# A new order of steps for linear attention and an expert layer on one core, with the first products of zeros 63 x 64 instead of 8 x 504

## The chip, the cores and the metric

The kernel runs on one core of one Trainium2 chip. The metric is the time of one execution on the device in microseconds (us). Three runs of the kernel before gave 184.23, 184.34 and 184.44; the median is 184.34. The profile is of another execution, which took 184.03 us; its span, from the first to the last instruction of the program, is 182.3 us.

A core has five engines with a queue each: PE (matrix products; its weight loads are shown as PEld), DVE (vector), ACT (scalar functions), POOL (general purpose) and SP, which here only issues DMA transfers. An engine takes its instructions strictly in their order and stops at the first whose inputs are not there.

## The reference

Part one is a gated linear recurrence over 4 batches, 8 heads, 768 time steps and a head size of 48. A state S of 48 x 48 per head is kept:

```
state = alpha[t][:, None] * state + outer(k[t], v[t])
y[t]  = q[t] @ state
```

Part two takes all y as a matrix x of 3072 tokens x 384 and computes, with weights 384 x 2048 and 2048 x 384 and two scalars s and b,

```
h = x @ w_in;  r = max(h, 0);  g = s * r * r + b;  out = g @ w_out
```

Everything arrives and leaves as float32; the kernel multiplies in bfloat16. It computes r * r @ w_out, multiplies by s afterwards, and adds b times the column sums of w_out.

## The kernel before

**Tiles.** The 768 steps of a batch are cut into 6 chunks of 128, which makes 24 blocks n of 128 tokens. The first 8 blocks are handled in 4 pairs m (two chunks of one batch, names that end in 2); the inputs, logarithms and sums of decay of the others are also shared by two blocks. Part two works on 12 groups g of two blocks, and on 8 units u of 256 columns of the hidden layer (one `mm1` step is one unit for one group).

**An order written out by hand.** There are no loops over the work. The text `PROGRAM` lists small steps, and the last lines of the kernel function call them one after the other. Each step emits its instructions to the queue of its engine, so `PROGRAM` fixes the order on every queue, and also which engine does a step that several could do (the word DVE, ACT or POOL at its end) and which PSUM bank it uses. Waits between engines follow from the data. The steps that the text speaks of, with their line in the profile:

- `ld2.x.m` and `ld1.x.n` (L294, L283) load alpha (a), q, k or v; `ld_i.i` (L307) and `ld_o.i` (L320) load quarters of w_in and w_out, 768 KB each; all stand in SP's queue. `st` writes results.
- `ln2`, `cum2` and `blk2` (two and eight products on PE), `eb2`, `ei2`, `el2` (exponentials on ACT) make the running decay; `mul2.q.m.s` and `mul2.k.m.s` (L447) scale q and k with it; `vc2` (L335 or L333) converts v.
- `T2` (eight products, L459) (`T2.m.x.bank`, x = 0 for q and 1 for k) transposes q or k into a bank, and `Tc2` copies the bank into tile qkT. From block 8 on, `T1.n` (L616) does both by a transposing DMA transfer.
- `A2` (16 products, L496) multiplies k and q of a pair; `mk2` (L509, on DVE) masks the result into tile am. `KV2` (16 or 8 products, L481) makes the states; `t1` (DVE) and `sn` (mostly POOL) advance them. `y2` (L544 and L556, 76 or 88 products) makes y, and `ye` copies y into tile xd. `A1`, `KV1`, `Ayy` are the same for single blocks.
- `mm1.g.u.w` (6 products, L732) is x @ w_in for unit u of group g into bank h_ps of number w; `re` (L742 on ACT, L744 on DVE) is the relu, `sq` the square into tile gt. `mm2.n.jq` (4 products, L766) is a quarter of the second matrix for block n; `oe` (L775) scales and adds the bias on DVE.
- `cih.i.h` converts half a quarter of w_in to bfloat16 and `co.i` a quarter of w_out (L333, L335). `cp`, `ca`, `cf` (L359) add up the columns of w_out; `bsm` and `bmm` (L379) spread s, b and these sums over the partitions, `bc` makes the bias tile. `mm2.0` needs `co.0`, and `oe.0` needs `bc`.
- `F.n.w.to` (L824) issues n products of zeros, w columns wide, into a bank that nobody reads. They compute nothing.

Every product on PE is a weight load and a product. `c_...` steps set constants.

```
def F(n, w, to):
    for _ in range(n):
        nc.tensor.matmul(
            out=bank[to][:, 0:w], lhsT=zeros[:, 0:128], rhs=zeros[:, 0:w], start=True, stop=True
        )

ops = dict(locals())
for item in PROGRAM.split():
    name, *args = item.split(".")
    ops[name](*(int(x) if x.lstrip("-").isdigit() else x for x in args))
```

Of the kernel before, what the change touches and what calls it, by code (L numbers as in the profile page):

```python
# [59 lines left out]
re.2.7.1.1.DVE mm2.2.2 ld1.v.10 t1.7 A2.3.1.a mm2.2.3 ld1.q.8 mk2.3.1 mm1.2.2.0 ld1.q.9 oe.1 y2.3 blk2.4  # L60
ld1.v.8 ye.6.DVE ye.7.ACT mm2.3.0 re.2.2.0.0.ACT oe.2 cumA.4 ld2.a.5 sq.2.2.0.POOL mm2.3.1 st.0 ei1.9
ei1.8 mm1.3.5.1 mul1.k.9.DVE ld1.v.12 sq.2.7.1.ACT mul1.k.8.DVE mm1.3.7.0 el2.4 re.3.5.1.2.ACT ld1.q.13
sn.7.POOL mm2.3.2 eb1.8 re.3.7.0.0.ACT mul1.q.8.DVE mm1.3.4.1 ln2.6 sq.3.5.2.DVE T1.8 mm2.4.0
re.3.4.1.1.DVE vc1.8.POOL eb1.9 mm2.3.3 vc1.9.POOL st.1 mul1.q.9.DVE KV1.8 mm1.3.6.0 t1.8 T1.9 mm1.3.1.1
re.3.6.0.2.ACT sq.3.4.1.DVE sn.8.POOL KV1.9 ln2.5 mm2.4.1 oe.3 st.2 c_U sq.3.7.0.ACT t1.9 mm1.3.0.0
ld2.a.7 re.3.1.1.1.ACT sq.3.6.2.DVE blk2.5 mm2.5.0 ld1.q.12 sn.9.POOL ld1.q.14 cumA.5 sq.3.1.1.DVE A1.8
vc1.10.POOL eb1.10 mm1.3.3.1 mk1.8 ei1.10 mm2.5.1 ei1.11 re.3.0.0.0.ACT mul1.k.10.DVE mm2.5.2 eb1.11
mul1.q.10.DVE re.3.3.1.2.ACT mm2.5.3 sq.3.0.0.DVE T1.10 sq.3.3.2.ACT mul1.k.11.DVE mm1.3.2.0
mul1.q.11.DVE KV1.10 oe.5 mm2.4.2 re.3.2.0.1.ACT T1.11 t1.10 el2.5 mm2.4.3 ln2.7 sq.3.2.1.POOL A1.9 oe.4
ld1.k.13 mm2.7.0 sn.10.POOL mk1.9 st.4 mm2.6.0 ld1.k.12 mm2.7.1 st.3 Ayy.10 ld2.a.11 ld1.v.13 mm2.6.1  # L70
ye.8.DVE ye.9.ACT vc1.12.POOL mk1.10 mm2.7.2 ld2.a.8 mm1.4.1.1 blk2.6 mm1.4.2.0 re.4.1.1.0.ACT
sq.4.1.0.DVE cumA.6 ld1.v.11 re.4.2.0.2.ACT A1.11 mm1.4.4.1 ei1.12 sq.4.2.2.DVE eb1.12 mul1.k.12.DVE
mm2.7.3 el2.6 re.4.4.1.1.ACT mul1.q.12.DVE mm2.6.2 eb1.13 mk1.11 T1.12 mm1.4.3.0 sq.4.4.1.DVE mm1.4.0.1
re.4.3.0.0.ACT mul1.q.13.DVE ld1.q.15 mm2.6.3 vc1.13.POOL ld1.v.14 re.4.0.1.2.ACT sq.4.3.0.DVE mm1.4.6.0
ei1.13 sq.4.0.2.DVE oe.6 KV1.12 mm1.4.7.1 re.4.6.0.1.ACT mul1.k.13.DVE mm2.8.0 vc1.11.POOL t1.12 T1.13
mm1.4.5.0 sq.4.6.1.DVE oe.7 Ayy.12 re.4.5.0.0.ACT ld1.q.16 ld1.k.14 ld2.a.9 mm2.8.1 ye.10.DVE ye.11.ACT
st.5 re.4.7.1.2.ACT sq.4.5.0.DVE blk2.7 mm1.5.4.0 mk1.12 ld1.k.15 KV1.13 mm1.5.5.1 re.5.4.0.1.ACT
sq.4.7.2.DVE mm2.9.0 t1.13 re.5.5.1.0.ACT mm1.5.6.0 sq.5.4.1.DVE sn.13.POOL ld1.v.15 A1.13
re.5.6.0.2.ACT cumA.7 vc1.14.POOL mk1.13 mm1.5.3.1 ld1.v.16 eb1.14 ei1.14 mm1.5.1.0 re.5.3.1.1.ACT
sq.5.6.2.DVE mul1.q.14.DVE mm2.8.2 el2.7 re.5.1.0.2.ACT mul1.k.14.DVE mm2.8.3 eb1.15 sq.5.3.1.DVE T1.14  # L80
ei1.15 sq.5.1.2.DVE mm1.5.2.1 sq.5.5.0.DVE mm2.9.1 re.5.2.1.1.ACT st.6 mul1.k.15.DVE mm1.5.0.0 oe.8
mm2.9.2 re.5.0.0.2.ACT vc1.15.POOL st.8 mm1.5.7.1 st.7 sq.5.0.2.DVE sq.5.2.1.DVE KV1.14 ld1.q.17
mm2.10.0 re.5.7.1.0.ACT t1.14 ln2.8 mm2.10.1 mul1.q.15.DVE mm2.10.2 sq.5.7.0.DVE T1.15 sn.14.POOL Ayy.14
ld1.k.16 mm2.10.3 ye.13.ACT mk1.14 vc1.16.POOL ld1.k.17 ye.12.ACT ld1.q.22 mm2.9.3 ld1.v.22 oe.10
mm1.6.1.0 blk2.8 KV1.15 re.6.1.0.2.ACT mm1.6.4.1 sq.6.1.2.DVE mm1.6.3.0 t1.15 re.6.4.1.1.ACT A1.15 oe.9
sn.15.POOL cumA.8 ld2.a.10 mm1.6.0.1 eb1.16 ei1.16 mul1.q.16.DVE mm2.11.0 re.6.0.1.0.ACT mul1.k.16.DVE
mm2.11.1 eb1.17 sq.6.4.1.DVE T1.16 ei1.17 sq.6.0.0.DVE mm2.11.2 re.6.3.0.2.ACT mul1.k.17.DVE mm2.11.3
el2.8 mk1.15 st.9 mm1.6.2.1 ld1.k.18 ld1.v.17 oe.11 mm1.6.6.0 re.6.2.1.1.ACT KV1.16 mm2.13.0
sq.6.2.1.DVE re.6.6.0.0.ACT t1.16 mm1.6.5.1 mul1.q.17.DVE mm1.6.7.0 sq.6.3.2.DVE T1.17 sn.16.POOL Ayy.16
re.6.7.0.1.ACT ln2.9 ld1.q.18 mm2.12.0 ye.14.ACT ye.15.DVE ld1.q.19 re.6.5.1.2.ACT sq.6.7.1.DVE ld1.k.19  # L90
mm2.13.1 ln2.10 ld1.v.18 sq.6.5.2.DVE mm1.7.0.0 sq.6.6.0.DVE st.10 mk1.16 mm1.7.4.1 vc1.17.POOL
re.7.0.0.1.ACT mm2.13.2 re.7.4.1.2.ACT blk2.9 sq.7.4.2.DVE mm1.7.6.0 ld1.q.23 A1.17 re.7.6.0.0.ACT
cumA.9 mk1.17 mm2.12.1 ei1.19 ld1.v.19 eb1.19 mm1.7.1.1 el2.9 sq.7.0.1.DVE eb1.18 mm2.13.3 ei1.18
mul1.q.18.DVE re.7.1.1.2.ACT mm1.7.7.0 mul1.k.18.DVE sq.7.1.2.DVE T1.18 mm1.7.2.1 mul1.q.19.DVE
re.7.7.0.1.ACT mul1.k.19.DVE mm2.12.2 re.7.2.1.2.ACT sq.7.7.1.DVE mm1.7.3.0 ld1.q.20 ln2.11 oe.13
vc1.18.POOL ld1.k.20 mm2.12.3 sq.7.2.2.DVE re.7.3.0.1.ACT T1.19 mm2.15.0 oe.12 KV1.18 vc1.19.POOL
mm1.7.5.1 ld1.q.21 sq.7.3.1.DVE mm2.14.0 t1.18 st.13 re.7.5.1.2.ACT ld1.v.20 mm2.14.1 st.12 Ayy.18 st.11
ld1.k.21 mm2.15.1 ye.16.ACT ye.17.DVE sq.7.6.0.DVE KV1.19 mm1.8.5.0 sq.7.5.2.DVE mk1.18 mm1.8.6.1
re.8.5.0.1.ACT blk2.10 mm1.8.7.0 re.8.6.1.0.ACT t1.19 A1.19 sq.8.6.0.DVE re.8.7.0.2.ACT cumA.10
sq.8.5.1.DVE mm1.8.3.1 sn.19.POOL mk1.19 el2.10 ei1.20 eb1.20 mm2.14.2 re.8.3.1.0.ACT mul1.k.20.DVE  # L100
# [761 lines left out]
```

## Time and profile before

| | |
|---|---|
| median of three runs | 184.34 us |
| profiled execution, its span | 184.03 us, 182.3 us |
| PE busy, products | 171.9 us (94%), 2309 |
| DVE, ACT, POOL busy | 136.6, 103.8, 47.2 us |
| DMA | 34.96 MB, mean 192 GB/s |
| instruction queue q8 | 18 packets, 0.29 MB |
| granted PE clock | 1.00 throughout |
| fillers `F` | 21 products, 5.7 us busy |

A row of a group names line, engine, operation, the tile written and the tiles read. "Idle before" is the time in which the engine had nothing to do, with what ended it; "issue" there means that no event in the profile explains the wait. A window's row lists the busy time of each engine in a stretch of the span, and the share of the 16 DMA engines. The chain of work that ended last is followed back from the last instruction. Where a line has x16, 16 instructions are merged.

### The profile page before, as it was taken

The page shows a single profiled execution, that of the slowest core. Times are in us where ns is not written, and L with a number is a line of the kernel's source. Part 1 is how long each engine was busy: PE and PEld are TensorE (multiplying, and loading weights), DVE is VectorE, ACT ScalarE, POOL GpSimd, SP SyncE. Part 2 cuts the span into 40 slices and gives each one's busy share as a digit, 9 for nine tenths or more (in the row PEclk, how much of TensorE's full clock was granted, in tenths as well). Part 3 has the DMA queues.
Part 4 walks back from the last instruction along what each step waited for, and adds up shares of the span by engine and source line. Part 5 has one row for each costly group of instructions (what it writes and reads, how often), then busy time and mean ns, then how long its engine had stood idle before and what let it go on. Part 6 is the DMA issues. An engine that isn't in the chain of part 4 may idle for free.

```text
span 182.3 us, 5580 instructions
## 1 busy us (share of the span) xinstructions
PE 171.9 (94%) x2309; PEld 122.5 (67%) x2309; DVE 136.6 (75%) x257; ACT 103.8 (57%) x204; POOL 47.2 (26%) x79
## 2 busy tenths in 40 slices
...
GB/s 156 325 355 375 276 338 374 365 271 212 196 217 211 156 158 260 163 234 155 214 238 202 190 223 153 151 214 185 250 58 154 79 96 150 2 5 86 0 133 86
DMA packets 101357, 34.96 MB, mean 192 GB/s; under 512 B 94548, under 2 KB 99796, under 8 KB 101332
## 3 DMA queue, kind: packets, MB, share of 16 engines
...
q8 instruction: 18, 0.29, 0.6%
...
## 4 chain that ended last, share of the span: by engine, by line
PE 75%; DVE 10%; DMA 6%; SPq 3%; issue 3%; POOL 1%; ACT 1%; DVEq 0%; POOLq 0%
PE o_ps L766 31%; PE h_ps L732 28%; SPq L294 3%; DMA qkT<-qk 3%; PE a_ps L638 3%; DMA k_in<-in_k_dram 3%; DVE colsum L359 3%; DVE am L509 2%; PE py_ps L660 2%; PE ct_ps L660 2%; PE ct_ps L571 2%; PE py_ps L625 1%; POOL qk L447 1%; DVE t L701 1%; DVE r L744 1%
## 5 line engine op out<-in xcount | busy, mean ns | idle before, releaser
L732 PE MATMUL h_ps<-xd,w_in_bf 128*128 128x256 bf16 x576 | 74.2, 273 | 0.8 <-DVE r L744 0.6
L742 ACT ACTIVATE r<-h_ps 128x512 bf16<-128x512 f32 x87 | 51.8, 599 | 40.7 <-PE h_ps L732 36.8
L766 PE MATMUL o_ps<-w_out_bf,gt 128*128 128x384 bf16 x368 | 69.3, 326 | 0.1
L732 PEld LDWEIGHTS <-w_in_bf 128*128 128x128 bf16 x576 | 54.6, 98 | 13.7 <-issue 2.9
L766 PEld LDWEIGHTS <-gt 128*128 128x128 bf16 x368 | 34.3, 98 | 19.4 <-issue 0.9
L761 DVE TENSOR_TENSOR gt<-r 128x512 bf16<-128x512 bf16 x74 | 34.3, 484 | 13.4 <-ACT r L742 12.8
L711 POOL TENSOR_TENSOR s_st<-t,blast 128x384 bf16<-128x384 bf16 x15 | 14.6, 971 | 38.8 <-DVE t L701 35.8
L647 DVE TENSOR_TENSOR am<-a_ps,U 128x1024 bf16<-128x1024 f32 x16 | 19.5, 1219 | 3.8 <-PE a_ps L638 3.7
L335 POOL CAST vp<-v_in 128x384 bf16<-128x384 f32 x18 | 11.6, 646 | 33.4 <-DMA v_in<-in_v_dram 24.4
L775 DVE SCALAR_TENSOR_TENSOR o_sb<-o_ps,bs,bias_w 128x384 f32<-128x384 f32 x23 | 14.1, 613 | 3.8 <-PE o_ps L766 2.2
L759 ACT ACTIVATE gt<-r 128x512 bf16<-128x512 bf16 x18 | 11.1, 628 | 3.8 <-DVE r L744 3.7
L333 ACT ACTIVATE xd<-ct_ps 128x384 bf16<-128x384 f32 x6 | 2.9, 490 | 15.2 <-PE ct_ps L660 8.6
L394 ACT ACTIVATE la<-a_in 128x768 bf16<-128x768 f32 x12 | 10.1, 841 | 2.4 <-DMA a_in<-in_alpha_dram 2.4
L761 POOL TENSOR_TENSOR gt<-r 128x512 bf16<-128x512 bf16 x4 | 4.7, 1164 | 23.3 <-ACT r L742 12.3
L595 DVE TENSOR_TENSOR qk<-k_in,binv 128x384 bf16<-128x384 f32 x16 | 9.7, 612 | 1.2 <-ACT binv L585 1.1
L509 DVE TENSOR_TENSOR am<-a_ps,mask 128x1024 bf16<-128x1024 f32 x6 | 7.3, 1223 | 3.9 <-PE a_ps L496 3.7
L595 DVE TENSOR_TENSOR qk<-q_in,b_s 128x384 bf16<-128x384 f32 x16 | 9.7, 606 | 0.6 <-ACT b_s L581 0.4
L701 DVE TENSOR_TENSOR t<-py_ps,s_st 64x192 bf16<-64x192 f32 x26 | 9.2, 353 | 0.9 <-PE py_ps L625 0.5
L335 DVE CAST xd<-ct_ps 128x384 bf16<-128x384 f32 x6 | 3.3, 556 | 5.1 <-PE ct_ps L660 5.0
L447 DVE TENSOR_TENSOR qk<-q_in,b_s 128x384 bf16<-128x384 f32 x7 | 3.8, 556 | 4.3 <-ACT b_s L424 4.3
L824 PE MATMUL a_ps<-zeros 128*128 128x504 bf16 (+3 forms) x17 | 5.7, 478 | 1.3 <-DVE zeros L215 1.3
L333 ACT ACTIVATE xd<-py_ps 128x384 bf16<-128x384 f32 x8 | 3.9, 487 | 5.0 <-PE py_ps L660 3.6
...
## 6 DMA issues: line engine op xcount, KB each, us to landing
...
```

The costliest lines, as they stand in the source:

```text
L335: {"DVE": nc.vector, "POOL": nc.gpsimd}[eng].tensor_copy(out=out, in_=in_)
L509: nc.vector.tensor_tensor(out=o, in0=i, in1=mask2[s].rearrange("a t p -> a (t p)").unsqueeze(1).to_broadcast([128, n, 128]), op=ALU.mult,)
L595: on(eng).tensor_tensor(out=half_of(qk, n)[:, "qk".index(x), :, 0:D], in0=half_of(ins[x], n).rearrange("a (h d) -> a h d", d=D), in1=half_ ...
L647: nc.vector.tensor_tensor(out=half_of(am, n).rearrange("a e p t -> a (e p) t"), in0=a_ps.rearrange("a e (p t) -> a (e p) t", t=128), in1=U ...
L701: nc.vector.tensor_tensor(out=t1_sb[n % 2][r, :, w], in0=p_ps[r, :, w], in1=s_sb[(n - 1) % 4][r, :, w], op=ALU.add,)
L711: on(eng).tensor_tensor(out=s_sb[n % 4], in0=t1_sb[n % 2], in1=bl.unsqueeze(2).to_broadcast([128, NP, 96]), op=ALU.mult,)
L732: nc.tensor.matmul(out=h_ps[w][:, i * n : (i + 1) * n], lhsT=w_in_bf[:, kk, 128 * j : 128 * (j + 1)], rhs=xd_sb[g % 3][:, kk, 0:n], start= ...
L742: nc.scalar.activation(out=r_sb[i], in_=h_ps[w], func=AF.Relu)
L759: nc.scalar.activation(out=unit_out(g, u), in_=r, func=AF.Square)
L761: on(eng).tensor_tensor(out=unit_out(g, u), in0=r, in1=r, op=ALU.mult)
L766: nc.tensor.matmul(out=o_ps[n % 2][:, 0:d_model], lhsT=gt_of(n)[:, j, c0 : c0 + C], rhs=w_out_bf[:, j, :], start=(j == 0), stop=(j == NJ - 1),
L775: nc.vector.scalar_tensor_tensor(out=out_sb[n % 3], in0=o_ps[n % 2][:, 0:d_model], scalar=s_col, in1=bias_w, op0=ALU.mult, op1=ALU.add,)
```

## The change

Only `PROGRAM` changes; every function is the same. All 89 lines of it are written anew (90 after). The steps that compute are the same set, apart from engine, bank and buffer of some; the order moves within some microseconds everywhere. The fillers go from 8 x 504, 1 x 240, 3 x 480, 2 x 480, 2 x 296 and 5 x 456 to 63 x 64, 8 x 64, 4 x 384, 5 x 432, 6 x 480, 2 x 296 and 2 x 480 columns: 69 more products. In the head, one of q's multiplies moves from DVE to POOL, `vc2` steps move to ACT and POOL, half of a weight conversion moves from DVE to POOL, and k of pairs 1 and 3 is loaded earlier against v. Counted over the program, `re` goes from 87 on ACT and 9 on DVE to 89 and 7.

```
-c_U2 ln2.0 ld2.q.1 c_ident F.8.504.a0 cum2.0.0 c_vp.0 ld2.v.0 ln2.1 blk2.0 c_mask2 cum2.0.1 eb2.0.0
-cum2.1.1 ld2.k.1 mul2.q.0.0.DVE eb2.0.1 cum2.1.0 ei2.0.0 blk2.1 mul2.q.0.1.DVE el2.0 ei2.0.1
-mul2.k.0.0.DVE ld2.v.1 F.1.240.a0 T2.0.0.c eb2.1.1 mul2.k.0.1.DVE ei2.1.0 T2.0.1.y Tc2.0.0.c.ACT ld_i.1
-mul2.q.1.1.POOL el2.1 Tc2.0.1.y.DVE eb2.1.0 ld_i.0 vc2.0.0.POOL ei2.1.1 F.3.480.a0 A2.0.1.o vc2.0.1.ACT
-mul2.q.1.0.DVE A2.0.0.a c_s.0 mk2.0.1.0 ld_o.1 mul2.k.1.0.POOL mk2.0.1.1 F.2.480.c T2.1.0.o0 mk2.0.0
-KV2.0 mul2.k.1.1.POOL Tc2.1.0.o0.ACT ld2.a.2 t1.0 c_t1.1 vc2.1.1.ACT F.2.296.c T2.1.1.o1 vc2.1.0.ACT
-y2.0 Tc2.1.1.o1.DVE ld2.v.2 t1.1 A2.1.1.o ye.1.ACT A2.1.0.a ye.0.ACT sn.1.POOL mk2.1.0 cih.1.1.ACT KV2.1
-c_V2 cih.1.0.ACT mm1.0.3.0 t1.2 ld2.q.2 mm1.0.2.1 mk2.1.1.0 sn.2.POOL re.0.3.0.0.ACT mk2.1.1.1
-cih.0.0.ACT cih.0.1.POOL t1.3 sq.0.3.0.ACT ld2.k.2 c_ones sn.3.DVE re.0.2.1.1.ACT F.5.456.a0 y2.1
-cp.1.DVE ld_o.0 mm1.0.1.0 ye.2.ACT ye.3.DVE ln2.2 mm1.0.0.1 co.1.DVE ld_i.3 sq.0.2.1.ACT cum2.2.1
...
-T2.2.0.c Tc2.2.1.y.ACT mm1.1.1.1 co.0.POOL Tc2.2.0.c.DVE sq.1.3.2.ACT KV2.2 re.1.1.1.0.DVE A2.2.0.a
-re.1.0.0.1.ACT ld_o.2 cp.0.POOL mk2.2.0 mm2.0.0 sq.1.1.0.ACT cih.3.0.ACT mm2.0.1 t1.4 A2.2.1.a
-cih.3.1.ACT mm1.0.6.1 sq.1.0.1.DVE ld2.v.3 sn.4.POOL mk2.2.1 mm1.0.7.0 ld_bs re.0.6.1.2.ACT cih.2.1.DVE
-mm1.1.7.1 re.0.7.0.0.ACT cih.2.0.DVE sq.0.7.0.ACT mm1.1.6.0 ld2.k.3 ca.0.1.DVE re.1.7.1.1.ACT y2.2
...
-mul2.q.3.0.DVE el2.3 re.1.4.0.2.ACT KV2.3 ca.0.2.DVE T1.6 sq.1.4.2.ACT mm1.2.4.0 sq.2.6.1.ACT cf.DVE
-re.2.1.1.0.DVE bmm ld1.q.11 ld1.q.10 sq.2.1.0.POOL mm1.2.7.1 bc ld1.k.10 oe.0 mm2.1.0 ld1.k.11
...
+ln2.0 ld2.q.1 c_vp.1 c_t1.0 F.63.64.a0 cum2.0.0 c_vp.0 ld2.k.1 ln2.1 blk2.0 c_mask2 cum2.0.1 eb2.0.0
+cum2.1.0 ld2.v.0 mul2.q.0.0.DVE eb2.0.1 cum2.1.1 ei2.0.0 blk2.1 mul2.q.0.1.DVE el2.0 ei2.0.1 ld_i.1
+mul2.k.0.0.DVE F.8.64.a0 T2.0.0.c eb2.1.1 mul2.k.0.1.DVE eb2.1.0 ei2.1.0 T2.0.1.y ld2.v.1
+mul2.q.1.1.POOL el2.1 Tc2.0.0.c.ACT Tc2.0.1.y.DVE ld_i.0 mul2.k.1.0.POOL ei2.1.1 F.4.384.a0 A2.0.1.o
+A2.0.0.a mk2.0.1.1 mul2.k.1.1.POOL vc2.0.0.ACT ld2.a.2 mk2.0.1.0 vc2.0.1.ACT mul2.q.1.0.POOL mk2.0.0
+F.5.432.c KV2.0 T2.1.1.o1 c_t1.1 t1.0 c_s.2 T2.1.0.o0 ld_o.1 Tc2.1.1.o1.ACT c_V2 Tc2.1.0.o0.DVE y2.0
+cih.1.0.ACT t1.1 ld2.v.2 A2.1.0.a A2.1.1.o ye.1.DVE sn.1.POOL vc2.1.1.ACT mk2.1.1.0 ye.0.ACT c_ones
+mk2.1.1.1 vc2.1.0.ACT cih.1.1.ACT ld2.q.2 F.6.480.h0 KV2.1 mm1.0.2.1 t1.2 cih.0.0.ACT ld2.k.2 mk2.1.0
+sn.2.POOL re.0.2.1.0.ACT F.2.296.o1 mm1.0.0.0 ln2.2 cih.0.1.POOL mm1.0.3.1 t1.3 re.0.0.0.1.ACT
+sq.0.2.0.DVE y2.1 ld_o.0 re.0.3.1.2.ACT sn.3.DVE mm1.0.1.0 cp.1.DVE ye.2.ACT ld_i.3 ye.3.ACT cum2.2.1
...
+re.1.3.0.0.ACT mul2.k.2.1.DVE el2.2 sq.0.0.1.ACT mul2.q.2.0.DVE F.2.480.o1 T2.2.1.y ld2.a.3 sq.1.2.2.DVE
+T2.2.0.c Tc2.2.1.y.ACT mm1.1.1.0 co.0.POOL Tc2.2.0.c.DVE vc2.2.1.ACT re.1.1.0.1.DVE A2.2.0.a
+sq.1.3.0.ACT KV2.2 mk2.2.0 ld_o.2 cp.0.POOL re.1.0.1.2.ACT mm2.0.0 ld_bs cih.3.0.ACT mm2.0.1 t1.4
+A2.2.1.a cih.3.1.ACT sq.1.0.2.DVE mm1.0.6.0 ca.0.1.DVE ld2.k.3 sq.1.1.1.ACT mm1.0.7.1 re.0.6.0.0.ACT
+sn.4.POOL mk2.2.1 re.0.7.1.2.ACT mm1.1.7.0 cih.2.0.POOL sq.0.7.2.ACT mm1.1.6.1 ld2.q.3 re.1.7.0.1.ACT
+cih.2.1.DVE y2.2 re.1.6.1.2.ACT cp.3.DVE ld2.a.6 sq.1.7.1.ACT mm1.1.5.0 sq.1.6.2.POOL ye.4.DVE ye.5.ACT
...
+mm1.2.4.0 ca.0.2.DVE vc2.3.0.ACT re.1.4.1.1.ACT KV2.3 ld1.k.8 cf.DVE sq.2.5.0.ACT mm1.2.1.1 ld1.v.9 t1.6
+re.2.4.0.0.ACT ld1.v.13 bmm sq.1.4.1.ACT mm1.2.7.0 bc oe.0 mm2.1.0 re.2.7.0.1.ACT st.0 sq.2.4.0.ACT
...
```

More of the change, by code (lines that the diff above doesn't have):

```diff
@@ L60 @@
[L60 to L100, printed above, removed]
@@ new lines @@
+sq.0.2.0.DVE y2.1 ld_o.0 re.0.3.1.2.ACT sn.3.DVE mm1.0.1.0 cp.1.DVE ye.2.ACT ld_i.3 ye.3.ACT cum2.2.1
+co.1.DVE sq.0.3.2.ACT cum2.2.0 blk2.2 eb2.2.1 mm1.1.2.1 ld_i.2 re.0.1.0.0.DVE vc2.2.0.POOL ei2.2.0
+sq.0.1.0.DVE re.1.2.1.2.ACT mm1.1.3.0 mul2.q.2.1.DVE ld_o.3 ei2.2.1 mm1.1.0.1 eb2.2.0 mul2.k.2.0.DVE
+re.1.3.0.0.ACT mul2.k.2.1.DVE el2.2 sq.0.0.1.ACT mul2.q.2.0.DVE F.2.480.o1 T2.2.1.y ld2.a.3 sq.1.2.2.DVE
+T2.2.0.c Tc2.2.1.y.ACT mm1.1.1.0 co.0.POOL Tc2.2.0.c.DVE vc2.2.1.ACT re.1.1.0.1.DVE A2.2.0.a
@@ new lines @@
+sq.1.5.1.DVE re.0.4.0.0.ACT mm1.0.5.1 cp.2.DVE eb2.3.1 ld1.k.11 mm1.2.0.0 sq.0.4.0.ACT co.2.POOL
+re.0.5.1.1.DVE ei2.3.1 cum2.3.0 re.2.0.0.0.DVE bsm sq.0.5.1.ACT blk2.3 ld1.k.9 mm1.2.6.1 bsc eb2.3.0
+mul2.k.3.1.DVE mm1.2.5.0 ei2.3.0 mul2.q.3.1.DVE ld2.a.4 re.2.6.1.1.ACT mm2.0.2 sq.2.0.0.DVE T1.7 el2.3
+sq.2.6.1.ACT mul2.q.3.0.DVE mm2.0.3 mul2.k.3.0.DVE re.2.5.0.0.ACT mm1.1.4.1 ca.2.3.DVE T1.6 vc2.3.1.ACT
+mm1.2.4.0 ca.0.2.DVE vc2.3.0.ACT re.1.4.1.1.ACT KV2.3 ld1.k.8 cf.DVE sq.2.5.0.ACT mm1.2.1.1 ld1.v.9 t1.6
```

98 lines of the change are left out of this document (66 added, 32 removed).

## The prediction

> **What bounds the kernel now.** I read the windows view first, cut where the stages change, because the page's 94% for PE is an average. Columns: window, length, then busy time and count on PE, PEld, DVE, ACT, POOL, the granted clock, DMA share and rate.
>
> ```profile
> 0.00:12.00 12.00, 9.57 (x96) 4.78 (x98) 5.84 (x18) 7.50 (x15) 7.29 (x28) 1.00 0.95 261
> 12.00:18.16 6.16, 3.59 (x152) 2.68 (x151) 3.46 (x7) 4.18 (x7) 3.98 (x9) 1.00 1.05 384
> 18.16:22.80 4.64, 3.71 (x110) 2.60 (x106) 4.53 (x9) 2.38 (x5) 1.77 (x4) 1.00 1.02 277
> 22.80:30.07 7.27, 7.19 (x96) 5.50 (x89) 6.77 (x14) 7.22 (x15) 3.09 (x2) 1.00 1.05 353
> 30.07:34.80 4.73, 4.64 (x57) 3.20 (x50) 4.56 (x8) 4.12 (x8) 2.23 (x2) 1.00 1.07 366
> 34.80:46.92 12.12, 11.23 (x188) 8.68 (x187) 12.09 (x20) 11.11 (x23) 4.13 (x3) 1.00 0.97 253
> 46.92:179.25 132.33, 132.01 (x1638) 95.08 (x1638) 98.96 (x187) 67.28 (x134) 24.70 (x33) 1.00 0.74 155
> 179.25:182.30 3.05, 0.00 (x0) 0.00 (x0) 0.41 (x1) 0.00 (x0) 0.00 (x0) 1.00 0.32 110
> ```
>
> From 46.92 us on PE has no hole: whatever brings it there earlier with the same work done is kept to the end. Before that four things take turns. DMA is full (share about 1) from the first transfers to 47 us; DVE is full from 18 to 47 us; PE does little until 22.8 us. Then the chain of work that ended last, between 14 and 48 us (start, length, what):
>
> ```profile
> 15.39 2.09 issue
> 17.48 0.31 PE a_ps L496 x5
> ...
> 46.30 0.57 DVE colsum L359
> 46.92 0.93 PE o_ps L379 x2
> 47.87 0.63 DVE bias_w L384
> ```
>
> PE stops for 2.09 us inside `A2.1.0.a`, after 11 of its 16 products, waiting for nothing that a semaphore would show; and DVE's sum of the weight columns (`cf`) releases `bmm` at 46.92. The DMA view of 15.2 to 15.4 us names the first:
>
> ```profile
> q8 instruction: 1, 0.02, 29.9%
> ```
>
> The queue of instructions moves one packet there, its first; the page has 18 with 0.29 MB, 16 KB each. Over PE's 4618 loads and products that is 63 bytes each, so a packet holds some 256 of them, 128 load-product pairs. Before the stall stand 223 pairs, so a block begins at pair 224; its packet ran from 15.28 to 16.23 and PE went on at 17.48. The next block begins with pair 352, the third product of `mm1.0.1.0`, whose packet ran at 20.8: there too PE slipped 0.1 us. Read as "a block is asked for when the one before it is entered", pair 96 (`KV2.0`, 11.97) asks and 17.48 receives: 5.5 us; next 17.48 to 23.13: 5.65 us.
>
> The DMA floor of this stage shows on POOL, and PE follows it at `mm2.0.0`:
>
> ```profile
> 26.98 2.58 POOL L335 CAST w_out_bf<-gt 128x1536 bf16<-128x1536 f32 x1 [5.39 <-DMA gt<-in_moe_w_out_dram]
> 29.52 1.81 POOL L359 TENSOR_TENSOR colsum<-gt 128x768 f32<-128x768 f32 x1
> ```
>
> **The change, part by part.** The 2288 products that compute something (2309 less 21 fillers) are the same; the rest is order, engines and fillers.
>
> *Fillers.* 8 of 504 and 63 of 64 are both 4032 columns. The old ones start 0.42 us apart (0.83 ns a column), so 64 columns are 53 ns, and 63 end near 4.8 us as now; `cum2.0.0` waits for `ln2.0` until 5.07. That needs a weight load to pass in less than 53 ns. Nearest row: `blk2.0`, 8 pairs from 5.64 to 5.84, 25 ns a pair. Bounds 0 (as there) and +3.4 us (63 loads in series at the 114 ns mean of their rows, 7.2 us); I take 0. `F.8.64` (8 x 25 to 53 ns, 0.2 to 0.4 us) begins at 7.11 like `F.1.240`, and nothing needs PE until 7.55: 0. `F.4.384` (0.64) replaces `F.3.480` (0.6), covered by the wait for qkT until 10.16. `F.5.432` (0.9) waits out `v`. `F.6.480.h0` (6 x 0.2 = 1.2) and the two later ones are costed below.
>
> *Blocks of instructions.* 55 more pairs at the start put the boundary at pair 224 into `y2.0` (40th product, near 14.1 us) and its request at `T2.0.0.c` (7.55). 7.55 + 5.5 = 13.0: the stall goes. The next boundary falls on the 18th product of `y2.1`: 14.1 + 5.65 = 19.7; the third on `mm1.1.1.0`: 20.3 + 6.0 (23.13 asked, packet at 26.95 + 0.9, 1.3 to use) = 26.3. Both are just in time by the sums below. The Trainium skill ("Runtime: NRT & Kernel Launch", Instruction fetch mechanics) says that blocks of 256 are fetched while the one before runs and that crossing is mostly hidden. By that rule moving boundaries would be worth 0; the trace agrees on the blocks and shows 2.09 us at the first crossing.
>
> *SP.* k.1 passes v.0, and the first w_in slice passes v.1. By landing times (q.1 9.0, next 10.2, 11.4) k.1 lands at 10.2 instead of 11.4, v.0 at 11.4; w_in slice 1 at 13.5 instead of 14.6, v.1 14.6 instead of 12.6. Everything to `ld_o.0` is the same set, so the POOL row above stays at 26.98. Later k.3, q.3 pass v.3 (about 1.1 us each); v.3 is needed last.
>
> *POOL, ACT and DVE, 9 to 20 us.* POOL takes q.1.0 from DVE: four multiplies of 0.99 from 9.18 end at 13.15. `T2.1.0.o0` ends at 13.75, `y2.0` 14.8 (now 14.8), `A2.1` both halves 15.45 (now 17.8). ACT then has Tc2 1.0, cih.1.0 0.8, vc 0.5, ye 0.5, vc 0.5 in a row from 13.35: 16.5. `F.6.480` covers that and ends at 16.7, so it costs 0.2. `KV2.1` ends 17.15 (now 18.1), `mm1.0.2` 17.85; the next waits for w_in slice 0 (landing 18.04, cast 0.8): 18.85 to 20.15 for two; `F.2.296` is hidden there. DVE's t1.3 ends near 19.8, so `y2.1` runs 20.15 to 21.3, now 22.80, and three `mm1` are done instead of two: 1.5 + 0.65 = 2.15 us ahead.
>
> *20 to 30 us.* `T2.2` waits for k.2 (lands about 24.9) and four DVE multiplies, so `F.2.480` is free; `KV2.2` and `A2.2.0` end near 28.4, now 30.07. Then `mm2.0.0` needs POOL's cast: 26.98 + 2.58 = 29.56. The lead is 0.5 us, and 1.2 us of the gain turn into a wait for that cast.
>
> *30 to 47 us.* DVE loses work: cih.2.0 to POOL (0.6), vc2.2 and vc2.3 elsewhere, `ye` and `sq` about even. In before DVE runs from 30.18 to 46.87 without a hole. In the new order `ca.0.1` follows POOL's sum (31.33), then `mk2.2.1` ends at 33.45, and what follows to `cf` adds up, in start-to-start times, to 11.8 (casts 2.7, column sums 4.0, three relus 1.9, four multiplies 1.9, the rest 1.3), with a 0.2 wait for `y2.2`: 45.5 against 46.87. On PE, `y2.2` ends at 35.15; ten `mm1` 6.55, two `mm2` 1.3, the rest 1.9 and a 0.7 wait for a relu on DVE give 45.6. So `bmm` starts 1.3 us earlier, if every estimate holds; I take 1.0, between this and the 0.5 at 30 us.
>
> *From 47 us.* Same PE work (132.0 us), relus 2 more on ACT. Counted in PE work, the nearest `mm2` behind its last `mm1` moves from 1.5 to 2.1 us, the shortest lead of a transpose over its reader from 4.4 to 4.7. I take 0. The end is the same 3.05.
>
> Sum: 184.03 (profiled; span 182.3) - 1.0 = 183.03. The median shown, 184.34, is 0.31 above that execution: **183.3 us**.
>
> **The rivals.** *More is kept:* the wider distances also remove holes after 47 us. PE's steps there run 0.65 per six or four products; at that pace the work is some 129.7, so 2.6 us are slack; half of it gives 182.0.
>
> *Nothing is left:* DMA pins `cf` through `ld_o.2` (landing 36.8) and k.3, q.3, and DVE, still full, stays where it was. For it: DMA share 0.97 to 47 us. Against: none of its four sums starts on a landing in before. 184.2.
>
> *The small products are paced by their loads (slower):* then the first stage ends 3.4 us later; `mm2.0.0`, 1.2 us early for its cast, would be 1.7 late against now, and DVE's saving returns 0.3: 185.7. It decides from about 90 ns a pair. Against it: 25 ns a pair at 5.64. The Trainium skill ("TensorE: Matmul & The Clock Gate", LDWEIGHTS) has a load take columns / 1.2 ns, 107 ns here. By that rule alone 63 of them would last 6.7 us, and the sum would be near this rival's; the 25 ns row speaks against it.
>
> *Late transposes (slower):* the chain holds one qkT transfer of 5.27 us at 80.7, which cost PE 0.38 at 85. The leads of T1.14 and T1.20 shrink from 5.4 to 4.7 us of PE work; five such transfers would each cost 0.5: 2.5 - 1.0 = +1.5, 185.8. It decides when transfers take over 4.9 us.
>
> **How the numbers follow.** Forecast 0.44 (its own range 182.8 to 184.0), more kept 0.20, nothing left 0.13, paced by loads 0.08, late transposes 0.15. A change under 0.2% (0.37 us) can't be told from none here. Faster: 0.44 less 0.02 near the edge, plus 0.20 and a little of "nothing left": 0.65. Within: 0.11. Slower: 0.24. The range leaves out the far half of both slower cases: 181.9 to 185.3.
>
> **What would show it.** No 2 us issue hole near 15 us in PE's timeline, `A2.1` done by 15.6; the first instruction packet at 8 to 12 us; `mm2.0.0` at about 29.6 behind POOL's cast; `bmm` at 45.6 to 46.4; PE busy throughout behind it. Wrong if `cum2.0.0` starts after 5.5, a new issue hole over 0.5 us stands in `y2.1` or `mm1.1.1`, or holes after 47 us add up to over 1.3 us.

## The result, and the profile after

The changed kernel takes 186.94 us (median of 20 runs, 185.22 to 189.84), the kernel before beside it 184.74 us: a ratio of 1.0108, with a 95% interval of 1.0082 to 1.0133. It was forecast 1.0 us faster and is about 2 us slower. The profiled execution took 187.66 us, its span is 185.9 us. Every line number is one higher than before, since `PROGRAM` has one line more. In all tables below a median takes in every execution, while the ratio compares only those in the record's fast state, so that a median can stand higher than its ratio says (g1, where two of twelve are left, and i2, where five are).

The windows of the changed kernel, with the columns of the prediction's first fence:

```profile
12.00:17.11 5.11, 4.62 (x148) 3.22 (x148) 4.87 (x10) 3.67 (x8) 4.39 (x12) 1.00 1.07 355
...
20.00:29.24 9.24, 8.18 (x173) 6.36 (x173) 8.28 (x15) 8.58 (x18) 2.76 (x4) 1.00 1.00 311
...
33.96:46.05 12.09, 11.14 (x187) 8.60 (x187) 11.91 (x20) 10.79 (x23) 3.02 (x2) 1.00 1.06 275
46.05:103.15 57.10, 53.05 (x650) 36.11 (x651) 39.48 (x75) 29.55 (x61) 13.22 (x19) 1.00 1.04 192
103.15:182.85 79.70, 79.65 (x988) 58.86 (x988) 55.49 (x110) 39.22 (x77) 9.98 (x14) 1.00 0.54 121
```

The head came out as worked out in this execution: PE is busy 4.62 of 5.11 us where the stall of 2.09 us was. `bmm`, the end of the head, starts at 46.05 (before: 46.92). The loss stands in the row from 46.05: PE is idle for 4.05 of 57.1 us between `bmm` and `Ayy.14`; before, it was idle for 0.32 us from `bmm` to the end of its work (the prediction's row of 46.92 to 179.25), 0.22 of them in front of `Ayy.12`. Behind 103 us it is full again. The chain of work that ended last names the holes (start, length, what):

```profile
81.76 5.34 DMA qkT<-qk
87.15 0.40 PE a_ps L639 x8
87.55 0.51 PE py_ps L661 x28
88.18 4.29 DMA qkT<-qk
92.51 0.40 PE a_ps L639 x8
...
97.23 5.88 DMA qkT<-qk
103.15 0.40 PE a_ps L639 x8
```

These are the transposing transfers T1.12, T1.13 and T1.14; each time PE goes on 0.05 us behind the landing. Another hole waits for T1.6, whose reader `A2.3.0.a` (L497) starts at 50.23 after 0.45 us of idle time. The view of waits (engine, line, what it waited for: us in total, times, longest) adds up those of the single blocks, first of the kernel before, then of the changed one:

```profile
PE a_ps L638 <- DMA qkT<-qk: 0.2, 1, 0.2
```

```profile
PE a_ps L639 <- DMA qkT<-qk: 3.5, 3, 1.8
```

Why they are late shows in SP's queue, first of the kernel before, then of the changed one (start, length of the issue; L616 and L617 are `T1`, L283 and L284 `ld1`, L294 and L295 `ld2`, L815 and L816 `st`):

```profile
80.69 3.34 SPq L616 DMA_TRANSPOSE qkT<-qk  x1
84.08 0.58 SPq L283 DMA_DIRECT2D q_in<-in_q_dram  x1
84.75 0.53 SPq L283 DMA_DIRECT2D v_in<-in_v_dram  x1
85.39 1.64 SPq L616 DMA_TRANSPOSE qkT<-qk  x1
...
94.02 1.39 SPq L616 DMA_TRANSPOSE qkT<-qk  x1
```

```profile
81.76 2.98 SPq L617 DMA_TRANSPOSE qkT<-qk  x1
84.79 1.22 SPq L816 DMA_DIRECT2D out_dram<-o_sb  x2
86.06 0.59 SPq L284 DMA_DIRECT2D q_in<-in_q_dram  x1
86.69 1.38 SPq L816 DMA_DIRECT2D out_dram<-o_sb  x2
88.18 1.30 SPq L617 DMA_TRANSPOSE qkT<-qk  x1
89.52 2.67 SPq L284 DMA_DIRECT2D k_in<-in_k_dram  x3
92.23 0.97 SPq L284 DMA_DIRECT2D v_in<-in_v_dram  x1
93.24 1.82 SPq L284 DMA_DIRECT2D q_in<-in_q_dram  x2
95.11 0.70 SPq L284 DMA_DIRECT2D v_in<-in_v_dram  x1
95.86 1.26 SPq L284 DMA_DIRECT2D k_in<-in_k_dram  x1
97.23 1.92 SPq L617 DMA_TRANSPOSE qkT<-qk  x1
```

The multiplies that T1.13 reads end at 83.37, a microsecond earlier than before (84.42). But SP stands behind T1.12, st.4, q.15 and st.5 and issues it at 88.18. T1.14 is ready at 95.78, issued at 97.23 behind eight loads, and lands at 103.11. Four of these loads (k.16, k.17, q.16, q.17) are read 10 us later or more; before, only q.16 of them stood in front.

### The profile page after: what moved, and what is told of

The parts are those of the page before. It is cut to its first block, busy times and chain, and to the rows that moved or that the text cites. A ratio compares the mean times of both kernels' runs of the same rounds, so it can differ in the third digit from the quotient of the medians.

```text
span 185.9 us, 5717 instructions
## 1 busy us (share of the span) xinstructions
PE 174.2 (94%) x2378; PEld 125.9 (68%) x2378; DVE 132.8 (71%) x252; ACT 105.8 (57%) x208; POOL 45.8 (25%) x80
## 4 chain that ended last, share of the span: by engine, by line
PE 61%; DMA 15%; SPq 11%; DVE 7%; ACT 2%; issue 2%; DVEq 0%; ACTq 0%
PE o_ps L767 25%; PE h_ps L733 24%; DMA qkT<-qk 11%; SPq L295 8%; DMA wst<-in_moe_w_in_dram 4%; PE a_ps L639 3%; SPq L321 2%; PE py_ps L661 2%; DVE colsum L360 2%; PE ct_ps L572 2%; PE ct_ps L661 2%; SPq L308 1%; DVE qk L448 1%; PE py_ps L626 1%; PE ct_ps L416 1%
## 5 line engine op out<-in xcount | busy, mean ns | idle before, releaser
L743 ACT ACTIVATE r<-h_ps 128x512 bf16<-128x512 f32 x89 | 52.4, 597 | 40.7 <-PE h_ps L733 32.3
L762 DVE TENSOR_TENSOR gt<-r 128x512 bf16<-128x512 bf16 x74 | 32.3, 452 | 9.6 <-ACT r L743 9.1
L712 POOL TENSOR_TENSOR s_st<-t,blast 128x384 bf16<-128x384 bf16 x15 | 14.0, 934 | 62.0 <-DVE t L702 39.5
L336 POOL CAST vp<-v_in 128x384 bf16<-128x384 f32 x17 | 9.8, 585 | 25.2 <-DMA v_in<-in_v_dram 11.4
L596 DVE TENSOR_TENSOR qk<-q_in,b_s 128x384 bf16<-128x384 f32 x16 | 8.8, 553 | 2.9 <-ACT b_s L582 2.8
L639 PE MATMUL a_ps<-qkT 64*128 64x128 bf16 x128 | 6.3, 218 | 3.5 <-DMA qkT<-qk 3.5
L639 PEld LDWEIGHTS <-qkT 64*128 64x128 bf16 x128 | 4.0, 94 | 7.6 <-DMA qkT<-qk 4.9
L336 DVE CAST xd<-py_ps 128x384 bf16<-128x384 f32 x5 | 2.8, 556 | 5.8 <-PE py_ps L661 5.2
L825 PEld LDWEIGHTS <-zeros 128*128 128x128 bf16 x90 | 5.3, 121 | 2.3 <-DVE zeros L216 1.3
```

Of the source, the lines that this page charges most:

```text
L336: {"DVE": nc.vector, "POOL": nc.gpsimd}[eng].tensor_copy(out=out, in_=in_)
L596: on(eng).tensor_tensor(out=half_of(qk, n)[:, "qk".index(x), :, 0:D], in0=half_of(ins[x], n).rearrange("a (h d) -> a h d", d=D), in1=half_ ...
L639: nc.tensor.matmul(out=a_ps[:, e, 128 * p : 128 * p + 128], lhsT=T[r, 1, p, :], rhs=T[r, 0, p, :], start=True, stop=True,)
L712: on(eng).tensor_tensor(out=s_sb[n % 4], in0=t1_sb[n % 2], in1=bl.unsqueeze(2).to_broadcast([128, NP, 96]), op=ALU.mult,)
L743: nc.scalar.activation(out=r_sb[i], in_=h_ps[w], func=AF.Relu)
L762: on(eng).tensor_tensor(out=unit_out(g, u), in0=r, in1=r, op=ALU.mult)
```

## The experiments

Theory S: the transposes are late because loads that are not urgent stand in front of them in SP's queue. Theory D: DMA is full up to 110 us, so a PE that comes early waits there in any order, and a reorder only moves the hole. All kernels compute the same; "SP" in a diff means the order in SP's queue.

### Fillers and SP's order exchanged whole

```diff
 e1: the changed kernel; SP from T1.6 to T1.17 in the order of before
 e2: the kernel before; SP from T1.6 to T1.17 in the changed order
 e3: the changed kernel
-F.63.64.a0 ... F.8.64.a0
+F.8.504.a0 ... F.1.240.a0
 e4: the kernel before
-F.8.504.a0 ... F.1.240.a0
+F.63.64.a0 ... F.8.64.a0
```

> The changed kernel, with SP's queue between T1.6 and T1.17 in the order of the kernel before; every other queue as changed. Theory A (the new SP order issues loads ahead of the transposing transfers while DMA is full, so T1.12 to T1.14 land late): the 3.5 us of PE waiting for qkT shrink to under 1 us, Ayy.14 starts near 99 instead of 103, and the time falls from 186.9 to 183.5 - 185. Rival B (the new order on DVE, ACT and PE makes the operands of the transposes late, whatever SP does) and rival C (the 69 additional products of zeros): 186.5 - 187.5, holes as they are.

> The kernel before, with SP's queue between T1.6 and T1.17 in the new order; every other queue as before. Theory A: 186.5 - 188, with waits for qkT of 2 - 4 us at A1.12 to A1.14. Rivals B and C: 184.7 within 0.4.

> The changed kernel, with its first two fillers as before (8 x 504 and 1 x 240 columns in place of 63 x 64 and 8 x 64). Theory A: 186.9 within 0.7, the wait for qkT stays; the stall for the first block of instructions comes back (some 2 us near A2.1 or KV2.1), of which at most 0.5 reaches bmm, because POOL's cast pins mm2.0.0 near 29.5. Rival C: 184.7.

> The kernel before, with its first two fillers as changed (63 x 64 and 8 x 64 columns). Theory: the 2.09 us hole in A2.1.0.a goes, y2.1 starts 1 - 2 us earlier, bmm 0 - 0.9 us earlier, and the time is 0 - 0.9 us less: 183.8 - 184.7. Rival C: over 186.

| kernel | us (median, range) | ratio to before, 95% |
|---|---|---|
| e1 | 189.01 (188.38 to 190.45) | 1.0191 (1.0145 to 1.0237) |
| e2 | 191.34 (188.93 to 191.91) | 1.0270 (1.0207 to 1.0334) |
| e3 | 185.43 (184.77 to 187.37) | 1.0002 (0.9968 to 1.0035) |
| e4 | 184.43 (183.61 to 186.17) | 0.9960 (0.9923 to 0.9996) |

e1 missed its expectation, and e2 is far worse than the changed kernel. A whole queue order under another order of the multiplies makes other loads late: in e1 v.11 is issued at 83.66 instead of 69.68, in e2 v.16 at 103.02 instead of 92.69. SP's order is matched to the order of its readers, so these two say nothing on single transposes. e4 shows the fillers alone: the stall in `A2.1` is gone, `bmm` starts at 46.63, and the kernel is 0.4% faster by its ratio (on this group's ratios see below). e3 spoke against theory S, since it has the transposes and loads of the changed kernel and was not slower; it is taken up again below.

### Head and rest exchanged; transposes moved ahead

```diff
 f0: the changed kernel itself
 f1: the changed order up to re.2.5 (43 us), all that is left as in before
 f2: before up to re.2.5, all that is left as in the changed order
 f3: the changed kernel, SP:
-st.2 T1.9 ... ld2.a.9 ld2.a.8 T1.12 st.4 ld1.q.15 st.5 T1.13
+T1.9 st.2 ... T1.12 st.4 T1.13 ld2.a.9 ld2.a.8 ld1.q.15 st.5
-ld1.k.14 ld1.k.16 ld1.k.15 ld1.v.14 ld1.q.17 ld1.q.16 ld1.v.15 ld1.k.17 T1.14 st.6 T1.15
+ld1.k.14 ld1.k.15 ld1.v.14 ld1.v.15 ld1.q.16 T1.14 st.6 T1.15 ld1.k.16 ld1.q.17 ld1.k.17
```

> The changed kernel itself, so that the runs of this group and the one with the old fillers stand beside it on one chip. Theory S (transposes stand too far back in SP's queue of the changed order, whatever the head does): 186.9 us, ratio 1.008 to 1.013, holes in front of Ayy.12, A1.13 and Ayy.14 that add up to 2.5 to 4 us. Theory D (the DMA rings are full until 110 us, so a PE that comes early only waits there, in any order): the same 186.9, but the hole's place differs from execution to execution. Theory T (it is the phase: the order is sound and only one unlucky overlap of loads and transposes made it slow on that chip): 184.5 to 185.7.

> The changed order up to the 43rd microsecond (the relu of unit 5 of group 2), and behind it all that is left in the order, on the engines and in SP's order of the kernel before. Theory S: the head's 0.9 us are kept and the holes go: 183.3 to 184.1 against 184.7 for before, ratio 0.991 to 0.997; no hole over 0.7 us behind 47 us. Theory D: the lead is waited away at the transposes: ratio 0.998 to 1.003. Theory T: 0.99 to 1.01, no prediction.

> The other half: the kernel before up to the same step, and behind it the changed order with its engines and SP's order. Theory S: the holes stay and the head's 0.9 us are missing: 187 to 188.5, ratio 1.013 to 1.020. Theory D: a head that is 0.9 us late eats only slack, 186.5 to 187.2, ratio 1.009 to 1.013. Theory T (as with the old fillers, which also gave a late head): 185 to 185.8, ratio 0.998 to 1.004.

> The changed kernel with one thing different: in SP's queue T1.9 stands ahead of st.2, T1.12 and T1.13 ahead of the loads of alpha 9 and 8, of q.15 and of st.5, and T1.14 ahead of the loads of k.16, q.17 and k.17, whose readers come 10 us later; all other queues are as they were. Theory S: T1.12 is issued at 80.5 instead of 81.8, T1.13 at 83.5 instead of 88.2, T1.14 near 95.8 with fewer loads in front; the holes of 1.5, 0.5 and 2.0 us shrink to under 0.8 us together: 183.5 to 185.0, ratio 0.994 to 1.002. Theory D: loads that are pushed back make other readers late: 186 to 188, ratio 1.006 to 1.017, with holes at v, k or alpha in place of those at the transposes.

| kernel | us | ratio |
|---|---|---|
| f0 | 186.80 (184.92 to 187.92) | 1.0072 (1.0033 to 1.0112) |
| f1 | 184.74 (183.61 to 188.10) | 0.9973 (0.9937 to 1.0008) |
| f2 | 187.02 (185.49 to 193.09) | 1.0080 (1.0051 to 1.0109) |
| f3 | 186.14 (184.98 to 188.31) | 1.0062 (1.0028 to 1.0096) |

The whole loss is in the order behind 43 us: with the old order there (f1) it is gone, and with the old head and the new rest (f2) it is all there. With or without the new head, the new rest costs the same, so nothing of the head's microsecond shows in the end. Against the expectations, f1 stands between the two theories, f2 below both theories, and f3 in the interval of theory D.

f3's profile shows both theories at work. The transposes came out as meant; here is its SP queue:

```profile
81.02 1.29 SPq L617 DMA_TRANSPOSE qkT<-qk  x1
...
83.91 1.24 SPq L617 DMA_TRANSPOSE qkT<-qk  x1
...
94.64 1.57 SPq L617 DMA_TRANSPOSE qkT<-qk  x1
```

From `bmm` to `Ayy.14` it takes 52.62 us, against 57.10 in the changed kernel and 55.49 in f0. But then v.16, pushed behind three loads, is late, and PE waits for its conversion on POOL (timeline of f3):

```profile
108.69 0.77 POOL L336 CAST vp<-v_in 128x384 bf16<-128x384 f32 x1 [3.05 <-DMA v_in<-in_v_dram]
...
109.52 0.33 PE L626 MATMUL py_ps<-vp,qk 128*128 128x96 bf16 x4 [0.66 <-POOL vp L336]
```

`Ayy.14` to `A1.17` takes 19.83 us instead of 18.05, so that 1.8 of the 2.9 us won against f0 are given back.

### The give-back mended, the dose given to before

```diff
 g2: f3, SP:
-T1.15 ld1.k.16 ld1.q.17 ld1.k.17 ld1.k.18 ld1.v.22 ld1.v.16
+T1.15 ld1.v.16 ld1.k.16
 (T1.16 ahead of a.10 and k.18; T1.17 ahead of q.19; T1.18, T1.19 ahead of q.22, v.21;
  v.22, k.23 behind T1.19)
 g3: the kernel before, SP:
-T1.14 st.6 st.8 st.7 ld1.q.17 T1.15 ld1.k.16 ld1.k.17
+ld1.q.17 ld1.k.16 ld1.k.17 T1.14 st.6 st.8 st.7 T1.15
 g4: e4, SP:
-ld1.q.14 T1.10 ... ld2.a.11 ld1.v.13 ld2.a.8 ld1.v.11 T1.12
+T1.10 ... ld1.v.11 T1.12 ld1.v.13 ld2.a.8
 (T1.14 ahead of v.16; T1.16 and T1.17 ahead of k.18; a.11 behind T1.13)
 g1: f1, SP:
-ld2.k.1 ld2.v.0
+ld2.v.0 ld2.k.1
```

> As f3 (transposes ahead in SP's queue of the changed kernel), but the stretch from 98 to 125 us is mended too: v.16 directly behind T1.15, T1.16 ahead of the loads of alpha 10 and k.18, T1.17 ahead of q.19, and the loads of v.22 and k.23, whose readers come 40 us later, behind T1.19. f3 had cured Ayy.12 and Ayy.14 and then lost 1.8 us between A1.15 and A1.17 (14.7 us against 12.9). Theory S (a transpose is late because loads that are not urgent stand in front of it, and their order can be mended): Ayy.14 at most at 100.3, A1.15 to A1.17 12.9 to 13.3 us, 184.2 to 185.3, ratio 0.994 to 1.001. Theory D (the rings are full, and every reorder only moves the hole): 185.7 to 187, ratio 1.003 to 1.010, with holes of over 0.7 us at another reader.

> The kernel before with one thing different: in SP's queue T1.14 stands behind the loads of q.17, k.16 and k.17, as in the changed order, instead of ahead of them. Theory S: T1.14 is issued near 96.2 instead of 94.0 and lands at 100.5 to 102 with three loads in front, Ayy.14 waits 0.8 to 2.3 us, and the end is as much later: ratio 1.003 to 1.012. Theory D: the leads are eaten elsewhere anyway: 0.998 to 1.002.

> The kernel before with the new first fillers (63 x 64 and 8 x 64, as in e4) and with transposes ahead in SP's queue: T1.10 ahead of q.14, T1.12 ahead of alpha 11, v.13 and alpha 8, T1.14 ahead of v.16, T1.16 and T1.17 ahead of k.18, v.22 behind. e4's profile had holes of 1.3 and 1.5 us at Ayy.10 and Ayy.12. Theory S: they go: 183.0 to 184.3, ratio 0.989 to 0.996, below e4's 0.996. Theory D: other readers take the holes over: 0.995 to 1.002.

> f1 (the changed order up to 43 us, the order of before behind it) with the loads of v.0 and k.1 in the old order. In f0, f1, f3 and e1 KV2.0 waited for v.0 until 13.2 us, against 12.0 in the kernel before; in the changed kernel's first profile it started at 12.1. Theory H (the head's gain is lost to v.0): KV2.0 at most at 12.2, y2.1 near 20.0, 0.3 to 0.8 us less than f1: ratio 0.992 to 0.996. Rival: y2.1 is set by the slices of w_in and by DVE and POOL, not by KV2.0, and k.1 a microsecond later costs what v.0 gains: as f1, 0.995 to 1.000.

| kernel | us | ratio |
|---|---|---|
| g2 | 184.96 (183.81 to 186.54) | 1.0019 (0.9983 to 1.0055) |
| g3 | 186.93 (185.48 to 192.58) | 1.0114 (1.0062 to 1.0166) |
| g4 | 185.65 (184.49 to 187.88) | 1.0049 (1.0014 to 1.0083) |
| g1 | 189.50 (185.14 to 190.75) | 1.0067 (1.0015 to 1.0120) |

g2 and g3 speak for theory S. With nothing changed but SP's order, g2 ends at 1.0019, a hair above the interval that S gave; the changed kernel had 1.0108, and 1.0072 as f0. And g3 makes the kernel before as slow as the changed one by setting T1.14 behind three loads, of which k.16 and k.17 now also stand in front of T1.15. Its SP queue and PE, by their timelines:

```profile
94.39 1.02 SPq L283 DMA_DIRECT2D q_in<-in_q_dram  x1
95.46 1.45 SPq L283 DMA_DIRECT2D k_in<-in_k_dram  x2
97.02 1.56 SPq L616 DMA_TRANSPOSE qkT<-qk  x1
```

```profile
98.68 1.63 PE L766 MATMUL o_ps<-w_out_bf,gt 128*128 128x384 bf16 x9
100.84 0.40 PE L638 MATMUL a_ps<-qkT 64*128 64x128 bf16 x8 [0.54 <-DMA qkT<-qk]
```

T1.14 is issued at 97.02, three microseconds after before, and PE waits for it. This execution took 185.48 us, the fastest of its six, and its hole at `Ayy.14` is 0.54 us; what the median lost beyond that, no profile shows.

g4 speaks for theory D: the same cure made e4 slower, by more than D gave. Its profile is of its longest execution (187.88 us), so it shows one way in which this happens and not the price. a.11, put behind T1.13, now stands in front of k.14 and k.15. DVE waits for k.15 before its multiply, and the square behind that on DVE keeps PE waiting (timeline of g4):

```profile
99.61 0.56 DVE L595 TENSOR_TENSOR qk<-k_in,binv 128x384 bf16<-128x384 f32 x1 [1.63 <-DMA k_in<-in_k_dram]
...
101.09 0.99 PE L766 MATMUL o_ps<-w_out_bf,gt 128*128 128x384 bf16 x5 [1.75 <-DVE gt L761]
```

What matters is thus which load a transpose passes, and who reads next behind the place to which the load goes. g1 came out above both of its expectations, with a wide interval; in its profile `KV2.0` starts at 11.89, as meant, but `y2.1` at 21.81, no earlier than in f1 (20.91). The order of v.0 and k.1 stays open.

### Loads that nobody needs for 25 us

```diff
 h1: e4, SP:
-... ld2.a.11 ld1.v.13 ... T1.12 ... ld1.k.14 ld2.a.9 st.5 ... T1.14 st.6 st.8 st.7 ... T1.17
+... ld1.v.13 ... T1.12 ... ld1.k.14 st.5 ... T1.14 st.6 st.8 st.7 ld2.a.9 ... T1.17 ld2.a.11
 h2: g2, SP: T1.6 ahead of k.9, k.11; T1.10, T1.11 ahead of q.12, k.12; a.9, a.10, a.11 later
 h3: f1 with the two moves of h1
```

> e4 (the kernel before with the first fillers 63 x 64 and 8 x 64) with two loads moved in SP's queue: alpha 9 (read at 113 us, loaded at 88) behind st.7, alpha 11 (read at 122, loaded at 77) behind T1.17. No other load changes its place. Theory S: one load less in front of T1.12 and of T1.14 each: T1.12 lands 0.5 to 1.2 us earlier, e4's hole at Ayy.12 is under 0.5 us; 183.4 to 184.2, ratio 0.991 to 0.996. Theory D (the rings are full, a moved load only moves the hole): 0.996 to 1.003.

> g2 with T1.6 ahead of k.9 and k.11, T1.10 and T1.11 ahead of q.12 and k.12, and the loads of alpha 9, 10 and 11 nearer to their readers at 113, 125 and 128 us. Theory S: g2's holes of 1.0 and 1.4 us at A2.3.0.a and Ayy.10 go, and nothing is late in their place: 183.3 to 184.5, ratio 0.992 to 0.999. Theory D: 1.001 to 1.007.

> f1 (the changed order up to 43 us, that of before behind it) with the same two moves as h1. If the head's order is worth the 1.0 us of the prediction and the rest is clean: 183.0 to 183.7, and 0.4 to 0.8 us less than h1, whose head is the old one with the new fillers. If the head's order is worth nothing over its fillers: within 0.3 us of h1. f1 against e4 stood at 0.9973 against 0.996, on two chips.

| kernel | us | ratio |
|---|---|---|
| h1 | 184.27 (182.48 to 186.62) | 0.9931 (0.9896 to 0.9965) |
| h2 | 185.71 (184.77 to 189.36) | 1.0032 (0.9992 to 1.0072) |
| h3 | 184.44 (183.69 to 185.16) | 0.9969 (0.9938 to 0.9999) |

h1 beats both kernels: the old order, the new first fillers, and two loads of alpha out of the crowded stretch. Its windows show PE with 0.22 us of idle time from `bmm` to `A1.15`:

```profile
46.50:104.05 57.55, 57.33 (x740) 39.88 (x741) 45.98 (x84) 29.85 (x60) 14.74 (x20) 1.00 0.92 193
```

h3 stands within 0.4% of h1 and on the wrong side of it: the new head's order shows no gain over the old head with the new fillers. h2 missed theory S and came out as D had it. No transpose is late in its profile up to `Ayy.14`, and that stretch takes 52.60 us. But PE waits 1.27 us at 36.5 us, because a `ye` stands on DVE behind a column sum that waits for its load. And it waits twice more just before `Ayy.20`: 0.17 us for a square on DVE, which had itself waited 1.80 us for a store, and 0.42 us for T1.20, which SP issued 1.1 us after its operands were there. What is left of the new order's loss has thus, in this execution, other causes beside the transposes, the head among them.

### The contradiction of e3

```diff
 i1: e3 again, beside i2: the changed kernel
 i3: g2 with the old first fillers
-F.63.64.a0 ... F.8.64.a0
+F.8.504.a0 ... F.1.240.a0
```

> e3 (the changed order with the first fillers 8 x 504 and 1 x 240), on one chip with i2. Theory S (the queue's order alone; the head shifts only by when the lead is lost): as i2 within 0.4 us, 186.4 to 187.2, ratio 1.006 to 1.012. Theory P (the phase of the head against the loads decides how long the transposes take): 1.2 to 1.8 us less than i2, ratio 0.998 to 1.003.

> The changed kernel, on one chip with i1. Both theories: ratio 1.007 to 1.012.

> g2 (the changed order, transposes ahead and loads behind in SP's queue) with the first fillers 8 x 504 and 1 x 240. Theory S: the stall of 1.4 us in A2.1 comes back and costs what it cost in the old order: 0.3 to 1.0 us more than g2, ratio 1.003 to 1.008. Theory P: nothing to act on, as g2 within 0.4 us, 1.000 to 1.004.

i1 gave 186.09 us (ratio 1.0071, 1.0033 to 1.0110), i2 188.23 us (1.0043, 0.9993 to 1.0094), i3 185.05 us (1.0008, 0.9962 to 1.0053). On one chip the changed order with the old fillers is as slow as with the new ones, so e3's 1.0002 does not hold up: the ratio of a group is less certain than its interval says. The kernel before, beside which e1 to e4 ran, had a median of 185.88 us there and of 184.69 to 185.29 in the groups of f to i; so e4's 0.9960 may be too low as well. i2 came out below its expectation, and i3 missed S's: in the new order the fillers bring nothing that shows (1.0008 against g2's 1.0019).

i1 and i3 are also the cleanest test of theory S. They ran side by side, and their steps, engines and fillers are the same; only SP's order differs. The order with transposes ahead and loads behind is 1.0 us faster by the medians, 1.0008 against 1.0071, which is nearly all that i1 loses against the kernel before.

i2's profile, of the same kernel, suggests why the head's microsecond is worth little. `bmm` starts at 50.62 there, 4.6 us later than in the first profile: `KV2.0` waited for v.0 until 14.39 instead of 12.08, and then PE's granted clock fell to 0.5 from 15.3 to 18.8 us (the window below shows the mean, 0.67).

```profile
14.00:18.00 4.00, 3.41 (x100) 2.82 (x103) 1.63 (x4) 2.56 (x5) 2.40 (x8) 0.67 1.11 367
```

Yet `Ayy.14` starts at 103.23, the changed kernel's 103.15 again. PE took 52.61 us in between and never waited: with the same order of SP, no transpose was late for a PE that came late itself.

| from `bmm` to `Ayy.14`, us | new order there | old order there |
|---|---|---|
| as changed, as before | 57.10, 55.49 (f0), 52.61 (i2), 56.33 (f2), 53.49 (e3), 53.32 (i1) | 52.81, 55.24 (e4), 52.51 (f1), 52.64 (g1) |
| loads moved away | 52.62 (f3), 55.13 (g2), 52.60 (h2), 52.62 (i3) | 52.52 (h1), 52.99 (h3), 56.21 (g4) |

Without holes the stretch takes 52.5 to 52.6 us in either order.

## Why the prediction was wrong

*Fillers: right.* 63 products of 64 columns run from 1.26 to 4.80 us, 8 of 504 ran from 1.26 to 4.80. The pairs start 53 ns apart, while the row of one weight load lasts 132 ns: up to three overlap. The rival "paced by their loads" is out. The Trainium skill ("TensorE: Matmul & The Clock Gate", LDWEIGHTS) has one load take columns / 1.2 ns, 107 ns here. One after the other, 63 loads would take 6.7 us by that estimate; here all passed in 3.5 us. This holds for the pace of the first microseconds, 0.83 ns a column, where `mm1` later takes 0.42; the clock of 1.00 "throughout" in the table of before is on record only from 5.6 us on.

*Blocks of instructions: right.* The first packet ran at 10.87, and its instructions were issued in `y2.0` at 14.26 without a wait; the next two were used in `y2.1` and `mm1.1.1.0`, also without a stall. All 20 profiles agree: in the 13 with the new first fillers the first packet runs at 9.65 to 10.99 us and no such hole follows; in the seven with the old ones it runs at 14.42 to 16.03, and PE stops for 1.35 to 2.57 us in `A2.1`. What this is worth in time rests on e4 alone, 0.4% in the old order, and there on a group with uncertain ratios.

*The head's 1.0 us: 0.87 in the first profile, but not by the head's order.* There `bmm` starts at 46.05, before at 46.92. In the eight other profiles with the new head and the new fillers (without g1) it starts at 46.64, 46.80, 46.87, 46.87, 47.33, 47.63, 48.45 and 50.62, so the median of all nine is 46.87; the first profile was a lucky one. The old head varies too: 46.92, 47.16, 47.99 and 48.18 with the old fillers (before, g3, e2, f2), but 46.50, 46.63 and 46.93 with the new ones (h1, e4, g4). So what the head gains comes with the fillers, and its new order adds nothing that shows. A step that failed there is SP's: v.0, passed by k.1, was put at 11.4. In the first profile its conversion on ACT did start at 11.50. But in f0 it could start only at 12.61, and `KV2.0` at 13.2 instead of 12.0; and the seven others lie at 12.57 to 13.82. In the three with the old fillers (e3, i1, i3) it is 11.42 to 11.51 again; why, stays open. The timeline of f0:

```profile
12.61 0.52 ACT L334 ACTIVATE vp<-v_in 128x384 bf16<-128x384 f32 x1 [2.17 <-DMA v_in<-in_v_dram]
```

*"From 47 us ... I take 0": wrong, and the step that decided.* It measured the lead of a transpose in PE work, from its place in `PROGRAM` to its reader. That takes SP to be there when the operands are. SP came 1.3, 4.8 and 1.5 us after them for T1.12, T1.13 and T1.14, and then the transfers took 5.34, 4.29 and 5.88 us, against a median of 2.8 us for those with no load under way (last section). Of T1.14 the prediction saw a lead that shrank from 5.4 to 4.7 us of PE work, not the loads that had moved in front. That SP's order makes the loss is shown by i1 and i3; how much of it each transpose makes, only profiles of single executions tell. The condition "holes after 47 us add up to over 1.3 us" was met: 0.61, 1.51, 0.49 and 1.98, 4.6 us together, counted like the prediction's 0.38 at 85 us as what a step took over its usual time; as idle time of PE they are 0.45, 1.35, 0.33 and 1.82. With this fell the premise that whatever brings PE to 47 us earlier is kept to the end: i2 came there 4.6 us later than the first profile and reached `Ayy.14` at the same time.

*The rival "late transposes": right in sign, and in mechanism for T1.12 and T1.14*, at a chance of 0.15. These took more than its 4.9 us; T1.13 with 4.29 made PE wait too, since it was issued late. Its price, five times 0.5, was too low for this execution (4.6 us). Its sum, 1.5 us slower, came near the 2.0 of all runs, but it counted on a gain of 1.0 in the head that most executions do not have. Its places were partly wrong: T1.20 was in time, T1.12 and T1.13 were not.

*"More is kept": out.* Its 2.6 us of slack behind 47 us do not exist up to `Ayy.14`: 52.81 us before, 52.5 without any hole. *"Nothing is left"* holds for the head's order, though not for its reason: in the first profile's chain the last landing before `cf` is that of a quarter of w_in at 29.70, not of `ld_o.2`, k.3 or q.3. What the profiles show is that the conversion of v.0 starts anywhere from 11.50 to 13.82 us, a spread of more than the gain.

*POOL's cast:* it started 0.7 us later than before (27.72 instead of 26.98, behind the landing of `ld_o.0`) but took 1.47 us instead of 2.58, and `mm2.0.0` started at 29.24 against 29.56 predicted.
